# wo loaded in rows of 32 KB by two queues and turned on VectorE, with a reordered chain between the layers, in a cached decode of two attention and two FFN layers

## The chip, the cores and the metric

The kernel runs on one core of a Trainium2 chip (trn2). The metric is the device time of one launch in microseconds (us). Three runs of the kernel before took 293.29, 294.82 and 295.31 us, median 294.82.

## What is computed

One token of each of four sequences (B = 4, D = 512) goes through attention, FFN, the same attention again with the same caches and weights, and the same FFN again. K and V caches hold 8 heads of 4096 positions of 128 numbers for each sequence, in bf16; 32 query heads share them four by four.

```python
def _A_ref(x, k_cache, v_cache, wq, wo):
    q = (x @ wq).reshape(B, Sq, Hq, Dh).transpose(0, 2, 1, 3)
    k = jnp.repeat(k_cache, rep, axis=1)
    v = jnp.repeat(v_cache, rep, axis=1)
    scores = jnp.einsum("bhqd,bhkd->bhqk", q, k) * (Dh ** -0.5)
    p = _softmax(scores, axis=-1)
    o = jnp.einsum("bhqk,bhkd->bhqd", p, v)
    return o.transpose(0, 2, 1, 3).reshape(B, Sq, Hq * Dh) @ wo

def _B_ref(x, w_gate, w_up, w_down):
    return (_gelu(x @ w_gate) * (x @ w_up)) @ w_down

x = A_x
x = x + _A_ref(_layernorm(x), A_k_cache, A_v_cache, A_wq, A_wo)
x = x + _B_ref(_layernorm(x), B_w_gate, B_w_up, B_w_down)
x = x + _A_ref(_layernorm(x), A_k_cache, A_v_cache, A_wq, A_wo)
x = x + _B_ref(_layernorm(x), B_w_gate, B_w_up, B_w_down)
```

A K or V head of one sequence is 1 MiB. wq and wo are 4 MiB each, the three FFN weights 1.75 MiB each.

## The kernel before

The sequences (batches 0 to 3 in the code) are worked through one after the other, and each of them through layer 0 and layer 1 (the two passes; `L` in the names). For a batch the eight K heads are loaded once and stay in SBUF for both layers. V heads are loaded for layer 0 and again for layer 1, but for the heads in `HELD` (line 22), which stay. K and V heads share twelve slots of 1 MiB (`KV`); at the very end the four parts of wq, which is then no longer needed, serve as four more.

The order of the work is made by a planner in the kernel's own code (class `Plan`). Each step is a node with an engine, an assumed duration and the nodes it needs. `run` picks the order on each engine and the slot of each load; `LEAD`, `PATIENCE` and the `DMA_` numbers at the top steer it. The instructions are then emitted in this fixed order, and each engine works through its own in order. All loads but that of x are issued by SP in the order wq, K of batch 0, the first half of wo, V of batch 0, the second half of wo, w_gate, w_up, w_down in two halves, and then for each further batch its K, its V for layer 0, and the V of the batch before it for layer 1. A load into a slot waits on SP until the last reader of the slot's old content is done: for a slot of K these are the score products of layer 1 (`sc`, line 415), for a slot of V the values products (`val`, line 485).

The steps that the change and the prediction touch:

- K heads are turned in place before the scores, six of eight by VectorE (`turn`, line 366) and heads 5 and 7 by TensorE (line 373) with ScalarE's copies (`kcopy`, line 379).
- Scores of four heads at a time (z = 0 and 1) go to `S_ps` (line 415). Softmax: maximum (line 421) and bias (lines 429 to 432) on VectorE, exp on ScalarE (line 438), a turn of the result (line 447) on VectorE, a swap on TensorE (line 455), a copy on ScalarE (line 463).
- Values: head by head in two halves of 16 products of 128 weights each, into `O_ps` (line 485); `oscale` (line 493) divides by the softmax sum and writes `OT`.
- Output projection (`proj` line 613, `half_out` 632, `half_sum` 639, `proj_last` 623): heads grouped by `groups`, into `R_ps`; `addback` (lines 646 and 647) turns the result and adds it to XT, the residual, which is held with D on the partitions.
- Layer norm (`ln_sq` line 500, `ln_mm` 506, `ln_mid` 512 and 513, `ln_var` 521 and 522, `ln_root` 529 and 530): squares on VectorE, then one product with a matrix of 1/512 for the sums of x and of its squares together, then mean, difference and variance on VectorE, and the root on ScalarE.
- FFN: `up` (line 655) for gate and up, `ffturn` (line 662), GELU on VectorE and ScalarE (lines 678 to 707), `down` (line 715), `addback`.
- Query of layer 1: `qmm` (line 538) in two halves, `qevac` on ScalarE (line 551), `qturn` (line 556), `qsplit` (line 595), `qrep` (line 605), `expand` (line 392).
- `rows` (lines 727 and 728) turns the residual for the output, `leave` (line 732) adds the last FFN and writes out.

Line 1004 holds products that only keep TensorE busy; their results are not read.

Of the kernel before, what the change touches and what calls it, by code (L numbers as in the profile page):

```python
# [21 lines left out]
HELD = ((), (7,), (7,), (7,))  # L22
HALVES = {(b, 1, j) for b in range(3) for j in range(8)} | {(3, 1, 6)}
# [7 lines left out]
DMA_FETCH = 1.5  # L31
DMA_LEAD = 4.0

PATIENCE = (0.5, 1.5, 0.7)
LEAD = {"tn1": -3, "val0": 1, "sc10": -2, "chain": 2, "sc11": -6, "sm00": 1, "os0": -6, "op": -2, "sm01": 11, "sm10": 10, "qx1": 4, "other": 5, "sc00": 2, "sm11": 8, "os1": -4, "tn0": -2, "sc01": 1}
EARLY = {("pt", 1): 60.0, ("su", 1): 60.0}
WINDOW = 3.413
WARM = 0.45
FILL = 0.7
SPIN = 0.22  # L40
STREAM = {"sc": 0.85, "qm": 0.85, "up": 0.75, "up2": 0.75, "kt": 0.21, "pw": 0.16, "qp": 0.11, "qn": 0.05,
          "su": 0.02, "lnm": 0.03, "xt": 0.1, "ys": 0.2, "dn": 0.38, "dn2": 0.38}


def stage(n):
# [13 lines left out]
    if n[0] in ("lnq", "lnm", "lnc", "lnv", "lnr", "up", "ft", "ga", "gb", "gy", "gc", "zz", "dn", "da", "qm", "qe",  # L59
                "qt", "qn", "qc", "qk"):  # L60
        return "chain"
# [3 lines left out]
class Plan:  # L65
# [149 lines left out]
    def warm(self, places):  # L215
# [3 lines left out]
        for n, _ in self.order:  # L219
# [16 lines left out]
            past.append((z, last, 0.72 * d if kind == "val" else d - 0.15 if kind in ("op", "op2") else STREAM.get(kind, 0.0)))  # L236
# [4 lines left out]
def kernel(  # L241
# [22 lines left out]
    FT = F // 4  # L264
    scale = float(Dh) ** -0.5
# [237 lines left out]
    def ln_mm(bs, nb):  # L503
        def emit():
            st = R_ps[1][:, 0:2 * CD * nb].rearrange("p (s k b) -> p s k b", s=2, k=CD)
            nc.tensor.matmul(st, lhsT=ones_mean, rhs=XS[:, :, :, bs], start=True, stop=True)
        return emit

    def ln_mid(bs, nb):
        def emit():  # L510
            st = R_ps[1][:, 0:2 * CD * nb].rearrange("p (s k b) -> p s b k", s=2, k=CD)
            nc.vector.tensor_reduce(out=mu[:, :, 0:nb], in_=st, axis=AX.X, op=ALU.add)
            nc.vector.tensor_tensor(out=xn[:, :, bs], in0=XT[:, :, bs],
                                    in1=mu[:, 0, 0:nb].unsqueeze(1).broadcast_to([P, CD, nb]),
                                    op=ALU.subtract)
        return emit

    def ln_var(nb):
        def emit():
            t = lt[:, 0:nb]  # L520
# [12 lines left out]
    def qmm(z, bs, nb):  # L533
# [7 lines left out]
        return emit  # L541

# [46 lines left out]
    def qsplit(z, b):  # L589
        def emit():  # L590
            if b:
# [17 lines left out]
    def proj(src, nb, heads, first, last):  # L609
        def emit():  # L610
            for j in heads:
                for i in range(4):
                    nc.tensor.matmul(R_ps[0][32 * i:32 * i + nb, :], lhsT=src[:, 4 * j + i, 0:nb],  # L613
# [4 lines left out]
    def proj_last(src, nb, heads, last):  # L618
        def emit():
            todo = [4 * j + i for j in heads for i in range(4)]  # L620
            for h in todo:
                for t in range(4):
                    nc.tensor.matmul(R_ps[1][32 * t:32 * t + nb, 0:P], lhsT=src[:, h, 0:nb],  # L623
# [36 lines left out]
    def ffturn(z):  # L660
        def emit():
            nc.vector.transpose(out=PD[:, 0:FT].rearrange("p (c x) -> p c x", c=CF),  # L662
                                in_=R_ps[z][:, 0:FT].rearrange("p (r c) -> p c r", c=CF))
        return emit

    def ff(nb):
        n = CF * nb
        at, ah = (0, n) if nb > 1 else (992, 984)
        d = PD[:, 0:FT].rearrange("p (c x) -> p c x", c=CF)[:, :, 0:nb]
        u = PD[:, FT:FT + n].rearrange("p (c b) -> p c b", c=CF)  # L670
        g = PF[:, at:at + n].rearrange("p (c b) -> p c b", c=CF)
# [19 lines left out]
    def gelu_y(nb, y):  # L691
        def emit():
            d, g, u, h = ff(nb)
            if nb == 1:
                nc.vector.scalar_tensor_tensor(out=g, in0=g, scalar=y, in1=d, op0=ALU.mult, op1=ALU.mult)
            else:
                nc.vector.tensor_tensor(out=g, in0=g, in1=y.unsqueeze(1).broadcast_to([P, CF, nb]),
                                        op=ALU.mult)
                nc.vector.tensor_tensor(out=g, in0=g, in1=d, op=ALU.mult)
        return emit  # L700

    def gelu_c(nb):
        def emit():
# [3 lines left out]
            nc.vector.tensor_tensor(out=h, in0=g, in1=u, op=ALU.mult)  # L707
        return emit

    def down(nb, k):  # L710
        def emit():
            h = ff(nb)[3]
            for c in range(7 * k, 7 * k + 7):
# [12 lines left out]
    def rows():  # L726
        nc.vector.tensor_copy(out=xp[:, :, 0:B], in_=XT)
        nc.vector.transpose(out=xrow.rearrange("p (r c) -> p c r", c=CD), in_=xp)
# [14 lines left out]
    def groups(b, L):  # L743

        g = [[0, 1, 2, 3], [4, 5], [6], [7]]
        if L:
            g = [[7], [6, 5, 4], [3, 2, 1, 0]] if b < B - 1 else [[0], [1, 2, 3], [7], [4, 5], [6]]
        return g
# [14 lines left out]
    def loads_v(b, L):  # L763
        heads = [j for j in sum(groups(b, L), []) if not (L and j in HELD[b])]
        for i, j in enumerate(heads):
# [19 lines left out]
            if halves:  # L785
                for m in range(2):
                    pl.load(name + (m,), 4.1, ld_part(name, m, src), rd[m], soft=soft[m], half=True)
# [6 lines left out]
    def ld_wo(n):  # L794
        return lambda pick: nc.sync.dma_start(
            out=wo_sb[:, 16 * n:16 * n + 16],
            in_=A_wo[2048 * n:2048 * n + 2048].rearrange("(h p) n -> p h n", p=P))

    def ld_wd(k):
        return lambda pick: nc.sync.dma_start(  # L800
            out=wd_sb[:, 7 * k:7 * k + 7], in_=B_w_down.rearrange("(q c) n -> q c n", q=P)[:, 7 * k:7 * k + 7])

    pl.load("x", 0.5, ld_x, None)
    pl.load("wq", 32, plain(wq_sb[:], A_wq, "(q c) n -> q c n"), None)
# [4 lines left out]
    pl.load("wg", 14, plain(wg_sb[:], B_w_gate, "(q c) n -> q c n"), None)  # L809
# [242 lines left out]
```

## Time and profile before

| | us |
|---|---|
| median of three runs | 294.82 |
| profiled execution | 291.89 |
| its span (first to last instruction) | 290.1 |
| TensorE products busy, of which line 1004 | 236.3, 67.7 |
| VectorE busy | 133.5 |
| ScalarE busy | 74.5 |

The profile is of one execution. Engines are PE (TensorE products), PEld (its weight loads), DVE (VectorE), ACT (ScalarE) and SP, which issues the loads here; "SPq" or "ACTq" is the issuing instruction itself. Times are us from the span's start. A row of the chain of waits has start, duration and what it was; the chain is followed back from the last instruction. A row of a group has the line, engine and operation, the tiles and shapes, the count, then busy us and mean ns of one, and then the idle time before them with what ended it. A row of a stretch has from and to, its length, the busy time of the engines with the number of instructions, the granted TensorE clock, the share of time in which the DMA engines were busy, and what they moved in GB/s. The share can be a little over 1, since packets of one DMA engine overlap. The line of digits has forty slices of 7.25 us, in tenths.

### The profile page before, as it was taken

To read this page: it belongs to the slowest core of one execution; us is meant where nothing else is said; L and a number is where in the kernel's file an instruction comes from. 1 tells how busy PE (TensorE), PEld (TensorE's weight loads), DVE (VectorE), ACT (ScalarE), POOL (GpSimd) and SP (SyncE) were. 2 spreads that over 40 slices of the span, in tenths; PEclk is the share of its full clock that TensorE was granted. 3 is DMA by queue.
4 is the path that set the end of the run, shared out by engine and by line. 5 is a ranking of instruction groups with operands and counts; after the bars stand their busy time and mean duration, and the time that the engine had idled before them with its cause. 6 is when DMAs were issued, how large, how long until landed. Compare 5 with 4: busy or idle time off the path is not lost.

```text
span 290.1 us, 9733 instructions
## 1 busy us (share of the span) xinstructions
PE 236.3 (81%) x4419; PEld 138.3 (48%) x4419; DVE 133.5 (46%) x380; ACT 74.5 (26%) x167; POOL 0.7 (0%) x6
## 2 busy tenths in 40 slices
PE   4988887878687888798888698879977889897794
PEld 1433454443233565455434465554445655565552
DVE  4149911002289942052389721343998213444034
ACT  1020751001023852101224731000338321113010
POOL 0000000000000000000000000000000000000000
PEclk9999999999999999999999999999999999999999
DMA  7999999999999999999999999999999999999910
GB/s 312 412 421 419 376 405 416 414 371 426 415 407 395 419 421 417 402 407 406 393 417 416 425 416 411 405 407 390 413 422 416 408 387 403 396 382 420 411 47 1
DMA packets 21657, 112.04 MB, mean 386 GB/s; under 512 B 2032, under 2 KB 6128, under 8 KB 12272
## 3 DMA queue, kind: packets, MB, share of 16 engines
q1 hardware_dynamic: 21568, 111.42, 95.3%
q8 instruction: 34, 0.56, 0.8%
q14 instruction: 7, 0.06, 0.0%
q10 hardware_dynamic: 48, 0.01, 0.0%
HBM read 111.42 MB, written 0.00 MB: 384 GB/s over the span
## 4 chain that ended last, share of the span: by engine, by line
DMA 62%; PE 16%; SPq 11%; DVE 7%; issue 2%; ACT 1%; DVEq 0%
DMA KV<-in_A_v_cache_dram 43%; DMA KV<-in_A_k_cache_dram 8%; SPq L351 7%; PE O_ps L485 7%; DMA wd_sb<-in_B_w_down_dram 6%; DMA wq_sb<-in_A_v_cache_dram 5%; SPq L741 3%; PE S_ps L415 3%; DVE KV L366 2%; PE R_ps L715 1%; PE R_ps L538 1%; DVE PA L662 1%; PE S_ps L1004 1%; PE R_ps L655 1%; DVE sm L421 1%
## 5 line engine op out<-in xcount | busy, mean ns | idle before, releaser
L485 PE MATMUL O_ps<-PA,KV 128*128 128x56 bf16 x1920 | 66.3, 188 | 20.8 <-DMA KV<-in_A_v_cache_dram 17.3
L485 PEld LDWEIGHTS <-KV 128*128 128x128 bf16 x1920 | 57.6, 97 | 40.8 <-DMA KV<-in_A_v_cache_dram 32.4
L1004 PE MATMUL S_ps<-iden_b 128*128 128x512 bf16 x226 | 67.7, 401 | 3.6 <-DVE iden_b L321 3.6
L366 DVE STREAM_TRANSPOSE KV<-KV 128x1024 int32<-128x1024 int32 x48 | 56.5, 1214 | 0.6 <-DMA KV<-in_A_k_cache_dram 0.4
L379 ACT ACTIVATE KV<-R_ps 128x512 bf16<-128x512 f32 x64 | 34.9, 595 | 28.0 <-PE R_ps L373 27.9
L415 PE MATMUL S_ps<-KV,PA 128*32 128x512 bf16 x384 | 35.3, 394 | 2.1 <-DVE KV L366 1.3
L1004 PEld LDWEIGHTS <-iden_b 128*128 128x128 bf16 x227 | 21.9, 107 | 27.6 <-issue 11.7
L373 PE MATMUL R_ps<-iden_b,KV 128*128 128x128 bf16 x256 | 22.1, 219 | 6.3 <-ACT KV L379 3.1
L421 DVE TENSOR_REDUCE sm<-S_ps 128x1 f32<-128x512 f32 x16 | 10.8, 677 | 27.4 <-PE S_ps L415 27.4
L373 PEld LDWEIGHTS <-KV 128*128 128x128 bf16 x256 | 15.8, 97 | 14.8 <-issue 10.2
L415 PEld LDWEIGHTS <-PA 128*32 128x32 bf16 x384 | 11.4, 94 | 13.2 <-issue 4.4
L493 DVE TENSOR_TENSOR OT<-O_ps,XS 128x4 bf16<-128x4 f32 (+1 forms) x12 | 2.0, 164 | 32.9 <-PE O_ps L485 32.9
L415 PE MATMUL S_ps<-KV,QN 128*32 128x512 bf16 x128 | 16.8, 381 | 0.2 <-ACT KV L379 0.2
L438 ACT ACTIVATE PA<-S_ps,sm 128x512 bf16<-128x512 f32 x16 | 11.7, 732 | 20.4 <-DVE sm L432 17.6
L632 ACT ACTIVATE PA<-R_ps 128x256 f32<-128x256 f32 x10 | 3.8, 384 | 46.2 <-PE R_ps L613 41.1
L529 ACT ACTIVATE sm<-sm 128x1 f32<-128x1 f32 (+1 forms) x10 | 2.0, 203 | 52.6 <-DVE sm L522 52.6
L493 DVE TENSOR_TENSOR OT<-O_ps,rdk 128x16 bf16<-128x16 f32 (+3 forms) x18 | 3.1, 170 | 26.7 <-PE O_ps L485 26.7
L463 ACT ACTIVATE PA<-T_ps 128x512 bf16<-128x512 f32 x16 | 9.6, 597 | 13.0 <-PE T_ps L455 11.8
L556 DVE STREAM_TRANSPOSE PA<-PA 128x256 int32<-128x256 int32 x10 | 4.4, 437 | 14.9 <-ACT PA L551 14.2
L613 PE MATMUL R_ps<-wo_sb,OT 128*1 128x512 bf16 (+1 forms) x124 | 8.7, 378 | 2.6 <-DMA wo_sb<-in_A_wo_dram 1.4
L646 DVE STREAM_TRANSPOSE PA<-R_ps 128x128 f32<-128x128 f32 x9 | 2.9, 317 | 16.5 <-PE R_ps L623 10.2
L447 DVE STREAM_TRANSPOSE PA<-PA 128x256 int32<-128x256 int32 x16 | 7.0, 434 | 7.5 <-ACT PA L438 7.5
(92 smaller groups left out, 173.9 us busy)
## 6 DMA issues: line engine op xcount, KB each, us to landing
KV<-in_A_v_cache_dram SPq DMA_DIRECT2D x34, 1024.0 KB, 15.0
KV<-in_A_k_cache_dram SPq DMA_DIRECT2D x32, 1024.0 KB, 13.5
KV<-in_A_v_cache_dram SPq DMA_DIRECT2D x46, 512.0 KB, 7.0
wq_sb<-in_A_wq_dram SPq DMA_DIRECT2D x1, 4096.0 KB, 12.2
wo_sb<-in_A_wo_dram SPq DMA_DIRECT2D x2, 2048.0 KB, 19.5
wq_sb<-in_A_v_cache_dram SPq DMA_DIRECT2D x4, 1024.0 KB
wg_sb<-in_B_w_gate_dram SPq DMA_DIRECT2D x1, 1792.0 KB
wu_sb<-in_B_w_up_dram SPq DMA_DIRECT2D x1, 1792.0 KB
```

The source lines that it names most:

```text
L351: nc.sync.dma_start(out=where[name], in_=src.rearrange("(p c) d -> p (c d)", p=P))
L366: nc.vector.transpose(out=w, in_=w)
L373: nc.tensor.matmul(R_ps[k % 2][:, P * u:P * u + P], lhsT=where[name][:, at:at + P], rhs=iden_b[:], start=True, stop=True)
L379: nc.scalar.activation(out=where[name][:, 512 * k:512 * k + 512], in_=R_ps[k % 2][:], func=ACT.Copy)
L415: nc.tensor.matmul(S_ps[z][32 * t:32 * t + 32], lhsT=w, rhs=k, start=(m == 0 and x == 0), stop=(m == 1 and x == 3))
L421: nc.vector.tensor_reduce(out=cms[:, z:z + 1], in_=S_ps[z][:].rearrange("p c r -> p (c r)"), axis=AX.X, op=ALU.max)
L438: nc.scalar.activation(out=PW[L][z].rearrange("p (a r e) -> p a r e", a=8, e=2), in_=S_ps[z][:].rearrange("p (a e) r -> p a r e", e=2), fu ...
L463: nc.scalar.activation(out=PW[L][z], in_=T_ps[z][:].rearrange("p t x -> p (t x)"), func=ACT.Copy)
L485: nc.tensor.matmul(Ov[L][:, j], lhsT=vw[:, c, :], rhs=w[:, c // 2, :, c % 2].unsqueeze(1).broadcast_to([P, WIDE, 4]), start=(m == 0 and c ...
L613: nc.tensor.matmul(R_ps[0][32 * i:32 * i + nb, :], lhsT=src[:, 4 * j + i, 0:nb], rhs=wo_sb[:, 4 * j + i, :], start=(first and j == heads[0 ...
L741: return lambda pick: nc.sync.dma_start(out=dst, in_=src.rearrange(pat, q=P))
L1004: nc.tensor.matmul(sinks[place].rearrange("p (a n) -> p a n", a=4), lhsT=iden_b[:], rhs=every, start=True, stop=True)
```

## The change

- wo is laid out in SBUF in another way. Before, partition p held row p of each of the 32 query heads, so that a load took rows of 1 KB. Now partition 32q + h gets the 32 rows 32q to 32q + 31 of head h, 32 KB without a gap, and a quarter q is one load into 32 partitions. SP issues quarters 0 and 2 before V of batch 0; ScalarE issues quarters 1 and 3 behind a one-column activation that reads K head 6. Eight instructions on VectorE then turn blocks of 32 by 32 (heads against rows) in place, each 1024 words of 4 bytes with a step of 1 KB, which gives the old layout. The projections of batch 0 wait for all eight. In VectorE's fixed order the first of the eight stands ahead of the turn of the second softmax half of layer 0 (line 447), the others behind it and ahead of all `oscale` of layer 0.
- V head 7 of batch 0 stays for layer 1 too, as in the other batches. It is not loaded again. The loads for batch 1 get three slots (K heads 0 to 2) before those of K of batch 0 come free; before they got four.
- Layer norm takes two products: that of x needs only XT, that of the squares goes to the end of `O_ps[0]`.
- The first half of the query of layer 1 (batches 0 to 3) is left in PSUM and turned there by VectorE, and `qsplit` reads PSUM; the copy on ScalarE is gone for this half. In VectorE's order a K turn of the next batch stands between the variance and this turn.
- In the FFN the gate's GELU is finished first, and the up product is turned in two parts (8 and 6 of 14 chunks); each is multiplied and goes into its part of the down product. w_down is loaded in the same parts.
- The turn of the rows for the output stands behind the variance. Head groups of the last output projection are split further.
- Planner constants are changed, and with them the order of independent steps throughout.

```diff
-HELD = ((), (7,), (7,), (7,))
-HALVES = {(b, 1, j) for b in range(3) for j in range(8)} | {(3, 1, 6)}
+HELD = ((7,), (7,), (7,), (7,))
+HALVES = {(b, 1, j) for b in range(3) for j in range(7)} | {(3, 1, 6)}
...
-PATIENCE = (0.5, 1.5, 0.7)
+PATIENCE = (0.3, 1.5, 1.0)
...
+    CUT = (0, 8, CF)
...
+    def ln_place(s, nb):
+        return O_ps[0][:, 512 - CD * nb:] if s else R_ps[1][:, 0:CD * nb]
+
+    def ln_mm(s, bs, nb):
+        def emit():
+            st = ln_place(s, nb).rearrange("p (k b) -> p k b", k=CD)
+            nc.tensor.matmul(st, lhsT=ones_mean, rhs=XS[:, s, :, bs], start=True, stop=True)
+        return emit
+
+    def ln_sum(s, nb):
+        st = ln_place(s, nb).rearrange("p (k b) -> p b k", k=CD)
+        nc.vector.tensor_reduce(out=mu[:, s, 0:nb], in_=st, axis=AX.X, op=ALU.add)
...
+    def qturn_apart():
+        nc.vector.transpose(out=R_ps[0][:], in_=R_ps[0][:])
...
-    def ld_wo(n):
-        return lambda pick: nc.sync.dma_start(
-            out=wo_sb[:, 16 * n:16 * n + 16],
-            in_=A_wo[2048 * n:2048 * n + 2048].rearrange("(h p) n -> p h n", p=P))
+    wo_rows = A_wo.rearrange("(h q c) n -> q h (c n)", q=4, c=32)
+
+    def ld_wo(q, queue):
+        queue.dma_start(out=wo_sb[32 * q:32 * q + 32].rearrange("p c n -> p (c n)"), in_=wo_rows[q])
+
+    def wo_beside():
+
+        nc.scalar.activation(out=sm[:, 25:26], in_=where["k", 0, 6][:, 0:1], func=ACT.Copy)
+        for q in (1, 3):
+            ld_wo(q, nc.scalar)
+
+    def wo_turn(k):
+        def emit():
+            w = wo_sb[:].rearrange("p c n -> p (c n)").bitcast(I32).rearrange("p (c n) -> p n c", c=32)
+            w = w[:, 32 * k:32 * k + 32]
+            nc.vector.transpose(out=w, in_=w)
+        return emit
...
-    pl.load(("wo", 0), 20.5, ld_wo(0), None)
+    for q in (0, 2):
+        pl.load(("wo", q), 15.7, lambda pick, q=q: ld_wo(q, nc.sync), None)
+    add("wa", "ACT", 0.9, [("k", 0, 6)], wo_beside)
     loads_v(0, 0)
-    pl.load(("wo", 1), 20.5, ld_wo(1), None)
...
+    wo_ready = [add(("wt", k), "DVE", 2.16, [("wo", 0), ("wo", 2), "wa"], wo_turn(k)) for k in range(8)]
...
-            return [(h, [("os", b, 0, i), ("wo", h[0] // 4)]) for i, h in enumerate(g)]
+            return [(h, [("os", b, 0, i)] + wo_ready) for i, h in enumerate(g)]
...
+    def ffn(tag, a, bs, nb, y, clear=None):
+
+        one = nb == 1
+        g = [None, None]
+        for z, w in ((0, wg_sb), (1, wu_sb)):
+            g[z] = add(("up", tag, z), "PE", 0.93, [a, g[0], "wu" if z else "wg"], up(z, w, bs, nb), ins=32)
+        t0 = add(("ft", tag, 0), "DVE", 0.65, [g[0]], ffturn(0))
+        a = add(("ga", tag), "DVE", 0.59 if one else 0.72, [t0, ("lnr", ("f", tag))], gelu_a(nb, y))
+        e = add(("gb", tag), "ACT", 0.22 if one else 0.25, [a], gelu_b(nb))
+        if not one:
+            a = add(("gz", tag), "DVE", 0.28, [a], gelu_z(nb, y))
+        e = add(("gd", tag), "DVE", 0.72 if one else 0.95, [e, a], gelu_d(nb, y))
+        t1, h, n = a, None, None
+        for k in range(2):
+            t1 = add(("ft", tag, 1 + k), "DVE", (0.44, 0.36)[k], [g[1], t1], ffturn(1, k))
+            h = add(("gh", tag, k), "DVE", 0.18, [t1, e, h], gelu_h(nb, k))
+            if k and clear:
+                add(("zz", tag), "DVE", 0.07, [h], clear)
+            n = add(("dn", tag, k), "PE", (0.55, 0.42)[k], [h, n, ("wd", k)], down(nb, k), ins=8 * (CUT[k + 1] - CUT[k]))
+        return n
```

More of the change, by code (lines that the diff above doesn't have):

```diff
@@ L519, in emit @@
         def emit():
+            ln_sum(1, nb)
             t = lt[:, 0:nb]
@@ L607, in qrep, with proj @@
         return emit
-    def proj(src, nb, heads, first, last):
+    def proj(src, cols, nb, heads, first, last):
         def emit():
```

172 lines of the change are left out of this document (84 added, 88 removed).

## The prediction

> **What bounds the kernel now.** I read the page's second and third part first.
>
> ```profile
> DMA  7999999999999999999999999999999999999910
> GB/s 312 412 421 419 376 405 416 414 371 426 415 407 395 419 421 417 402 407 406 393 417 416 425 416 411 405 407 390 413 422 416 408 387 403 396 382 420 411 47 1
> ```
>
> The 16 DMA engines are busy in all slices but the first and the last two: the kernel is one stream, in the order in which SP issues it, and then a tail of some 12 us without DMA. Two slices dip without going idle (376, 371), so I looked at those stretches by themselves.
>
> ```profile
> core 0: us, PE busy (x) PEld busy (x) DVE busy (x) ACT busy (x) POOL busy (x), PEclk, DMA share, GB/s
> 5.00:10.00 5.00, 4.87 (x29) 1.81 (x27) 1.27 (x8) 0.41 (x2) 0.00 (x0) 1.00 1.04 446
> 33.00:37.00 4.00, 3.35 (x48) 2.18 (x46) 2.92 (x5) 4.00 (x9) 0.00 (x0) 1.00 1.10 352
> 42.00:57.00 15.00, 12.69 (x251) 7.59 (x246) 2.33 (x9) 1.38 (x3) 0.00 (x0) 1.00 1.01 418
> 59.00:63.00 4.00, 3.12 (x44) 1.84 (x43) 0.16 (x1) 0.00 (x0) 0.00 (x0) 1.00 1.09 348
> 86.00:89.00 3.00, 2.22 (x34) 1.00 (x26) 2.57 (x9) 1.05 (x3) 0.00 (x0) 1.00 0.86 339
> 36.00:64.00 28.00, 23.29 (x391) 13.58 (x390) 2.65 (x11) 5.86 (x12) 0.00 (x0) 1.00 1.04 400
> ```
>
> The last column is the rate. 5 to 10 us is wq (rows of 32 KB), 33 to 37 and 59 to 63 the halves of wo (rows of 1 KB), 42 to 57 V heads (rows of 8 KB). From 86 to 89 us the engines are really short of work (share 0.86). Why they are is in the chain of waits and in SP's own row.
>
> ```profile
> 61.10 17.76 DMA wd_sb<-in_B_w_down_dram
> 78.90 0.59 PE R_ps L715 x28
> ...
> 80.07 0.18 DVE XS L500
> 80.29 0.40 PE R_ps L506 x2
> ...
> 82.22 0.61 ACT PA L551
> 82.85 0.46 DVE PA L556
> ...
> 84.33 2.31 DVE KV L366 x2
> 86.64 0.59 DVE sm L421
> ```
>
> ```profile
> 86.42 3.08 SPq L351 DMA_DIRECT2D KV<-in_A_k_cache_dram  x4
> ```
>
> This is the point on which everything hangs. All 12 slots are full: K of batch 0 holds eight until both layers' scores are done, the first four K heads of batch 1 hold the rest. SP issues the fifth only at 86.42, when the second score product of layer 1 ends. That product comes 7.5 us after the second half of w_down landed (78.90), and w_down lands when 29.25 MiB (wq 4, K 8, wo 4, V 8, the three FFN weights 5.25) have passed. So: release = landing of w_down + 7.5 us. What is issued behind the release is a fixed amount, and the end follows the release.
>
> **The change, part by part.**
>
> *wo in rows of 32 KB.* The 4.19 MB lie ahead of w_down before and after. At 350 GB/s they take 12.0 us; at wq's 446 they would take 9.4, at the 418 of 8 KB rows 10.0. I take 9.7, so w_down lands 2.3 us earlier (2.0 to 2.6), at 76.6. This supposes that a transfer into 32 partitions runs like one into 128; no row shows such a transfer, and the first rival is about that.
>
> *Two quarters on ACT's queue.* The new node stands in ACT's order behind 14 of the 16 copies of turned K.
>
> ```profile
> 34.53 4.87 ACT L379 ACTIVATE KV<-R_ps 128x512 bf16<-128x512 f32 x9
> ```
>
> So it runs at 39.4. With one more us of issue and first bytes, quarters 1 and 3 start at about 41, beside the V heads that SP has queued. Alone they would take 4.7 us, at an equal share of the engines 9.4: they land between 46 and 51, I take 48.5. The last two copies wait behind this node for under 1 us; the scores that need them, and all that follows them on PE, come later by at most that, with V loads queued until 52: nothing.
>
> *Eight transpositions of wo on VectorE.* No row shows one that strides by 1 KB on both sides. The nearest:
>
> ```profile
> L366 DVE STREAM_TRANSPOSE KV<-KV 128x1024 int32<-128x1024 int32 x48 | 56.5, 1214 | 0.6 <-DMA KV<-in_A_k_cache_dram 0.4 <-issue 0.2
> ...
> L646 DVE STREAM_TRANSPOSE PA<-R_ps 128x128 f32<-128x128 f32 x9 | 2.9, 317 | 16.5 <-PE R_ps L623 10.2 <-PE R_ps L715 6.3
> ...
> L728 DVE STREAM_TRANSPOSE PA<-PA 128x128 f32<-128x128 f32 x1 | 0.4, 408 | 0.0
> ```
>
> Of the same size, unstrided: 1.21 us. L646 reads with a stride, L728 writes with one, and L728 takes 91 ns longer for 128 elements, which is 0.73 us for 1024. So 1.21 (stride free), 1.94 (write pays), 2.67 (both pay); I take 1.94, since L646 pays nothing visible for its stride. Eight are 15.5 us (9.7 to 21.4). VectorE is idle for it (2.65 us busy between 36 and 64), but in its order stand behind them the turn of the second softmax half (0.43, between the first and the second), and all scalings of the outputs of layer 0. They end at 48.5 + 0.4 + 15.5 = 64.4. From there the path to the second half of the down product has: scaling 0.2, values of head 6 (they wait for that scaling, both on O_ps) 1.1, the first two projections 1.7, then from head 7 on what batch 3 shows in the chain without a wait for weights:
>
> ```profile
> 241.54 1.04 PE O_ps L485 x32
> 242.58 0.68 PE R_ps L623 x32
> ...
> 250.03 0.57 PE R_ps L715 x26
> ```
>
> That is 9.1 us from 241.54 to 250.60, plus some 1.5 us because the two half sums and one more projection now stand behind head 7: 13.6 in all, so 78.0 against 76.6 + 0.5 = 77.1 if w_down sets it. In batch 3 PE took values of another head between these steps, some 0.4 us of it in the path, which I take off: I put 0.5 us on the path (0 with free strides, 5.7 with 2.67 us each). The break-even is 1.9 us a piece; every 0.1 us above costs 0.8. A second place: PE's swap of that softmax half waits behind the first transposition (about 51.3), and the slots of V heads 5 to 7 behind it; the stream has work until about 54.3 and gets V head 5 issued at about 53. That is just enough; if not, up to 1 us.
>
> *V head 7 of batch 0 kept.* One load (2.5 us at 418 GB/s) less. But the slot it keeps is the one that K head 3 of batch 1 had. Ahead of the release the stream now has one MiB less to move, and behind it the same 73 MiB as before. The stall at 86 to 89 grows by what the load saved: net 0. It pays only as far as the release itself comes earlier (bounds -2.5 and +0.5).
>
> *Layer norm in two products, query turned in PSUM, gate ahead.* The sum product starts with the row of XT instead of its square: 0.2 us (80.07 to 80.29) earlier, in every chain. The query's copy and turn (0.61 + 0.46) become one turn in PSUM of 512 elements, about 0.7 by
>
> ```profile
> L662 DVE STREAM_TRANSPOSE PA<-R_ps 128x448 f32<-128x448 f32 x10 | 6.5, 648 | 7.2 <-PE R_ps L655 7.1
> ```
>
> but a 1.2 us K turn stands ahead of it in VectorE's order, behind the later variance steps, and ends about 0.6 us after the query product; before, ACT's copy hid this. 0.3 saved, 0.6 waited: nothing, or -0.3. Gate ahead changes the order of the same steps; turning the up product in two parts adds about 0.1 us and lets the first 8 of 14 down chunks start earlier: even. Per chain -0.2, in the release too.
>
> *Later stalls.* Slices of 402, 390, 387, 396 and 382 GB/s fall where batches 2 and 3 wait for the same kind of release. V in halves explains about 407; what is below is worth some 2.6 us in all. Four chains that are 0.2 shorter and a new order give perhaps -0.5 (between -2.6 and +1: planner constants were changed, and any order can lose).
>
> *The tail.*
>
> ```profile
> 280.68 0.17 DVE XS L500
> 280.85 0.10 DVE PA L727
> 280.97 0.41 DVE PA L728
> 281.38 0.17 DVE sm L512
> ...
> 281.81 0.96 PE R_ps L655 x16
> ...
> 286.12 0.98 PE R_ps L715 x56
> ```
>
> L727 and L728 stand in the chain; now the copy falls into the product's time, and the turn behind the variance. The reduction starts 0.3 us earlier. From the gate product to the end of the down product it was 5.3 us; with the new order I count 5.4. Tail: -0.25.
>
> **Sum.** -2.3 (wo) + 0.5 (transpositions) + 0 (head 7) - 0.2 (chain ahead of the release) - 0.5 (later) - 0.25 (tail) = -2.75 us. The profiled execution took 291.89 us (span 290.1), so its like would take 289.1; it stood 2.9 below the median of the three runs, and on that median, 294.82, the sum gives 292.1.
>
> **The rivals.**
>
> *A quarter of the partitions takes half the rate.* Every large transfer in this trace fills 128 partitions. If a transfer into 32 reaches only half of the paths into SBUF, the rate is 223 instead of 446 and a quarter takes 4.7 us instead of 2.35. SP's quarters run alone between 32 and 41 us, ACT's start as they end, so "two at once" doesn't happen. SP's two then lose 4.7 us for sure, ACT's two lose between 0 and 4.7, as V rows fill in or not. w_down lands 2.4 to 7.1 later than now; the transpositions are hidden then. 294.82 + 4.7 - 0.95 = 298.6 (296.3 to 301). It decides from 290 GB/s over wo downward. Against it: nothing in the trace. The Trainium skill, page "SBUF — State Buffer", section "Door 1: The DMA port swizzle", gives 189 GB/s for 1 MiB into partitions 0 to 31 and 328 into 128, because 32 partitions reach 8 of 16 ports, and says under "Can I just issue two DMAs to hit both halves?" that a second transfer adds 6%; by that, this rival is the outcome. No run here shows it yet.
>
> *The transpositions come late.* With 2.4 us each the path gains 3.7 instead of 0.5: 295.3. Speaks for it: two strided sides. Against it: L646.
>
> *Head 7 pays.* If the release comes earlier than I have it (weights landing sooner, the path shorter), the stall doesn't grow and 2.5 us are kept: 289.6. For it: only 7.5 us lie between landing and release, of which 2.3 is K turns ahead of the scores.
>
> **How the numbers follow.** Forecast 0.45, half rate 0.26, head 7 pays 0.17, late transpositions 0.12. The time is the forecast's, 292.1, its own range 290.4 to 293.8. The range for 8 in 10 runs from 288.9 (head 7 pays, a little more) to 298.6 (the middle of the half rate). The runs before spread over 0.7%, so less than 1% can't be told from no change: faster means under 291.87, slower over 297.77. The forecast lies at that edge: 0.22 faster, 0.23 the same. With head 7 (0.17) faster is 0.39; with 0.08 of the late transpositions the same is 0.31; the half rate and the rest of the late ones are slower, 0.30.
>
> **What would show it.** wo: its stretch at 420 to 446 GB/s, w_down's products at about 77; half rate: a stretch near 220 from 32 us on, with DMA share at 1. Transpositions: a group of 8 near 1.94 us, ending near 64. Head 7: one load less, and the stretch behind K head 2 of batch 1 idle for about 3 us. Tail: the turn of the rows no longer ahead of the reduction. The forecast is wrong if the release is not 1.5 to 2.5 us earlier than 86.4, or if the stretch behind it is not the same length.

## The result, and the profile after

The changed kernel is slower. Its median is 306.58 us (305.41 to 307.13, four runs) against 294.06 us of the kernel before in the same comparison; the ratio is 1.0458, with a 95% interval of 1.0418 to 1.0497. The forecast was 292.1 us, its range ended at 298.6. The profiled execution took 307.13 us with a span of 305.2; before, the span was 290.1.

First the DMA rows and the clock row of the profile after, in 40 slices of 7.63 us.

```profile
PEclk9999988559999999999999799999997999999999
DMA  8999998999996899999999999999999999899920
GB/s 318 398 421 426 290 251 180 273 398 366 427 417 283 309 418 422 413 410 408 400 404 424 417 418 417 408 389 343 421 414 422 413 413 394 320 394 416 413 79 2
```

The DMA engines are as busy as before, but in slices 5 to 8 (30.5 to 61 us) they move 290, 251, 180 and 273 GB/s. A high share of busy time with 180 to 290 GB/s instead of some 420 is the first thing to see: the engines did not wait for work, their packets were slow. Slices 13 and 14 (283, 309) are another matter: there the share falls as well. The same places as stretches (from and to, length, busy times, clock, share, GB/s):

```profile
5.00:10.00 5.00, 4.79 (x35) 1.99 (x33) 1.33 (x9) 0.42 (x2) 0.00 (x0) 1.00 1.01 433
...
50.00:58.00 8.00, 0.00 (x0) 0.00 (x0) 0.00 (x0) 0.00 (x0) 0.00 (x0) 0.57 0.95 196
60.00:65.00 5.00, 4.31 (x73) 3.24 (x71) 5.00 (x4) 0.60 (x1) 0.00 (x0) 0.50 1.01 419
97.00:100.00 3.00, 2.82 (x58) 1.47 (x55) 2.66 (x5) 0.18 (x1) 0.00 (x0) 1.00 0.10 38
```

wq, 32 KB rows into 128 partitions, runs at 433 GB/s. From 50 to 58 us ScalarE's quarters of wo and some V rows run at 196 with a share of 0.95, and TensorE does nothing. At 60 the stream is back at 419; at 97 to 100 it is dry. Now the chain of waits of the same stretch, and the group and SP rows that belong to it.

```profile
40.35 19.13 DMA wo_sb<-in_A_wo_dram
...
61.82 0.30 DVE PA L448
62.13 14.63 DVE wo_sb L842 x7
...
78.31 21.29 DMA KV<-in_A_k_cache_dram
```

```profile
L842 DVE STREAM_TRANSPOSE wo_sb<-wo_sb 128x1024 int32<-128x1024 int32 x8 | 16.9, 2192 | 14.3 <-DMA wo_sb<-in_A_wo_dram 14.3
```

```profile
L846 SPq DMA_DIRECT2D wd_sb<-in_B_w_down_dram x2: 432/454/475, 71.7 to 72.2; - x2
...
DMA to landing us min/median/max: 18.6/19.3/20.0
```

```profile
99.73 5.70 SPq L352 DMA_DIRECT2D KV<-in_A_k_cache_dram  x5
```

ScalarE's quarters, issued at 40.0, land at 59.5. The transpositions take 2.19 us each and end at 76.8. SP issues the second half of w_down at 72.2, and it lands 20.0 later, at 92.2 instead of 78.9. The release (the load that waits for the last score product of layer 1) comes at 99.73 instead of 86.42: 13.3 us later, of the 15.1 by which the span grew. The chain as printed runs from wo through the transpositions to a K head whose slot comes free behind them, and so seems to blame the transpositions; the run without them, below, says how much of the time they make.

### The profile page after: what moved, and what is told of

It reads as the page before. It is cut to its first block, busy times and chain, and to the rows that moved or that the text cites. A ratio compares the mean times of both kernels' runs of the same rounds, so it can differ in the third digit from the quotient of the medians.

```text
span 305.2 us, 9824 instructions
## 1 busy us (share of the span) xinstructions
PE 239.0 (78%) x4451; PEld 147.3 (48%) x4451; DVE 152.0 (50%) x409; ACT 71.7 (23%) x164; POOL 0.7 (0%) x6
## 4 chain that ended last, share of the span: by engine, by line
DMA 65%; PE 17%; DVE 11%; issue 3%; ACT 2%; SPq 0%; ACTq 0%; DVEq 0%
DMA KV<-in_A_v_cache_dram 36%; DMA KV<-in_A_k_cache_dram 19%; PE O_ps L486 7%; DMA wo_sb<-in_A_wo_dram 6%; DVE wo_sb L842 6%; DMA wq_sb<-in_A_wq_dram 4%; PE S_ps L416 4%; PE R_ps L374 2%; DVE KV L367 1%; ACT KV L380 1%; PE R_ps L746 1%; PE R_ps L637 1%; PE R_ps L557 1%; DVE sm L422 1%; PE R_ps L647 1%
## 5 line engine op out<-in xcount | busy, mean ns | idle before, releaser
L486 PE MATMUL O_ps<-PA,KV 128*128 128x56 bf16 x1920 | 68.1, 190 | 33.2 <-DMA KV<-in_A_v_cache_dram 26.1
L486 PEld LDWEIGHTS <-KV 128*128 128x128 bf16 x1920 | 60.7, 98 | 51.1 <-DMA KV<-in_A_v_cache_dram 34.4
L1059 PE MATMUL S_ps<-iden_b 128*128 128x512 bf16 x227 | 63.4, 396 | 3.6 <-DVE iden_b L322 3.6
L416 PE MATMUL S_ps<-KV,PA 128*32 128x512 bf16 x384 | 36.8, 416 | 2.3 <-DVE PA L393 1.8
L374 PE MATMUL R_ps<-iden_b,KV 128*128 128x128 bf16 x256 | 23.9, 231 | 6.5 <-DMA KV<-in_A_k_cache_dram 4.3
L842 DVE STREAM_TRANSPOSE wo_sb<-wo_sb 128x1024 int32<-128x1024 int32 x8 | 16.9, 2192 | 14.3 <-DMA wo_sb<-in_A_wo_dram 14.3
L374 PEld LDWEIGHTS <-KV 128*128 128x128 bf16 x256 | 17.3, 103 | 13.7 <-issue 6.7
L494 DVE TENSOR_TENSOR OT<-O_ps,rdk 128x4 bf16<-128x4 f32 (+2 forms) x19 | 3.2, 166 | 17.2 <-PE O_ps L486 17.2
L688 DVE STREAM_TRANSPOSE PA<-R_ps 128x448 f32<-128x448 f32 (+2 forms) x15 | 7.3, 490 | 6.0 <-PE R_ps L679 6.0
L469 PEld LDWEIGHTS S_ps<-mask_th,sm 128*128 128x128 f32 x32 | 4.8, 187 | 10.6 <-ACT PA L439 10.6
L469 PE MATMUL S_ps<-mask_th,sm 128*128 128x16 f32 x32 | 6.2, 269 | 4.8 <-ACT PA L439 4.6
```

The lines of the kernel that those rows point to most:

```text
L374: nc.tensor.matmul(R_ps[k % 2][:, P * u:P * u + P], lhsT=where[name][:, at:at + P], rhs=iden_b[:], start=True, stop=True)
L416: nc.tensor.matmul(S_ps[z][32 * t:32 * t + 32], lhsT=w, rhs=k, start=(m == 0 and x == 0), stop=(m == 1 and x == 3))
L469: nc.tensor.matmul(S_ps[z][:, 0, 0:16], lhsT=sms[:, z:z + 1].broadcast_to([P, P]), rhs=mask_th[:].rearrange("p t h -> p (t h)"), start=Tru ...
L486: nc.tensor.matmul(Ov[L][:, j], lhsT=vw[:, c, :], rhs=w[:, c // 2, :, c % 2].unsqueeze(1).broadcast_to([P, WIDE, 4]), start=(m == 0 and c ...
L688: nc.vector.transpose(out=PD[:, 32 * c0:32 * c1].rearrange("p (c x) -> p c x", x=32), in_=R_ps[z][:, 0:FT].rearrange("p (r c) -> p c r", c ...
L842: nc.vector.transpose(out=w, in_=w)
```

## The experiments

Theory A: a transfer into 32 neighbouring partitions runs at half rate. Theory B: the wait for wo and its transpositions costs the time. Ratios are against the kernel before, run beside each kernel. "Release" is SP's issue as above. Each kernel is the changed one in its own order with only what is named altered, but for four: two hold transfers alone, one is the kernel before with the wo part, and one has another plan for V head 7.

**wo as one transfer.**

```diff
-        queue.dma_start(out=wo_sb[32 * q:32 * q + 32].rearrange("p c n -> p (c n)"), in_=wo_rows[q])
+        if q == 0:
+            queue.dma_start(out=wo_sb[:].rearrange("p c n -> p (c n)"), in_=wo_rows)
```

ScalarE's two loads are deleted.

> As the changed kernel, in the same order of instructions, but wo comes as one transfer of 4 MiB from SP's queue into all 128 partitions, in the same rows of 32 KB, ahead of V of batch 0; ScalarE issues nothing of it. Theory A (a transfer into 32 partitions runs at half rate, and V rows beside it too; in the changed kernel's trace the stream moves 200 to 230 GB/s from 32 to 58 us): wo moves at 440 GB/s from 32 to 42 us, w_down has landed at 75.3 us (77.6 before, 89.4 in the changed kernel) and the release, the issue of K head 3 of batch 1 (99.7 in the changed kernel), comes at 84.2 to 85.5; with the 205.5 us behind it that gives 291 to 293 us. Theory B (the eight transpositions, now 2.19 us each, and what waits for them set the release; there are 40.2 us from the landing of wo to the release): the transpositions end at 59 to 60 us, but the release stays behind the weights, later than 90 us, and the time is over 297.

Measured: 357.41 us, ratio 1.2176 (1.2117 to 1.2236). Neither theory had the reason ("over 297" of theory B covers the number alone). The DMA row and a stretch of this kernel's trace:

```profile
DMA  8999992222223999799999999999999999999940
```

```profile
60.00:100.00 40.00, 0.00 (x0) 0.00 (x0) 0.00 (x0) 0.00 (x0) 0.00 (x0) 0.50 0.25 61
```

wo alone ran for 40 us with a share of 0.25, that of four engines out of sixteen, and 61 GB/s, 15 for each of the four. The source pattern has the four quarters as its outermost step. The Trainium skill, page "DMA: Bandwidth & Descriptors", section "Why a DMA increments its semaphore by 16 and not by 1", says that the number of engines is the largest up to 16 that divides the slowest dimension of both patterns: four here, and the share agrees. So this run is no test of either theory, but it holds a hint: each of the four engines moved little more than half of what each of sixteen moves in wq (433 / 16 = 27 GB/s).

**All four quarters on SP.**

```diff
-        pl.load(("wo", q), 15.7, lambda pick, q=q: ld_wo(q, nc.sync), None)
+        pl.load(("wo", q), 15.7, lambda pick, q=q: [ld_wo(q + i, nc.sync) for i in range(2)], None)
```

ScalarE's two loads are deleted.

> As the changed kernel, but all four quarters of wo are issued by SP, one after the other ahead of V of batch 0; ScalarE issues none. Theory A in its narrow form (only the quarters themselves run at half rate): wo takes 18.8 us instead of 9.4, nothing runs beside it, V of batch 0 then moves at 418 GB/s, w_down lands at about 84.5 us, 5 us earlier than in the changed kernel, where the V rows of ScalarE's two quarters were slowed as well: about 301.5 us. Theory B: wo has landed at 51.5 us instead of 59.5, the release comes 8 us earlier: 298.5. If two queues at once had been a help, this kernel would be slower than the changed one: over 307.

Measured: 304.26 us, ratio 1.0356 (1.0300 to 1.0412), release at 96.66.

```profile
34.00:52.00 18.00, 10.72 (x83) 5.15 (x81) 2.27 (x6) 6.48 (x14) 0.00 (x0) 0.77 0.99 206
55.00:65.00 10.00, 6.26 (x94) 4.47 (x95) 8.41 (x5) 0.60 (x1) 0.00 (x0) 0.54 1.01 412
```

With nothing beside them the quarters run at 206, and V comes at 412 as soon as they are through. Theory A in its narrow form had the mechanism, but 2.8 us too little: w_down landed 3.1 us earlier than in the changed kernel, not 5. This run alone does not part the theories, since wo landed at 56.5 us (not 51.5), 3.0 earlier than in the changed kernel, and a release that follows wo would have come 3 us earlier too. The next run parts them. "Two queues at once" was no help: its release comes 3.1 us later than this one.

**Without the transpositions.**

```diff
-            nc.vector.transpose(out=w, in_=w)
```

> As the changed kernel with its four quarters on two queues, but the eight transpositions of wo on VectorE are left out, so wo stays in the layout in which it was loaded and the output is not the reference's. Theory A: w_down lands no more than 0.5 us earlier than at 89.4 and the time is that of the changed kernel, 306.6, or up to 1 us less. Theory B: what waits behind the last quarter's landing is 17 us shorter, V heads 5 to 7 and the FFN weights are issued up to 6 us earlier, and the release comes 6 us earlier or more: 300 or less.

Measured: 305.54 us, ratio 1.0434 (1.0358 to 1.0511), release at 98.14, 1.6 us earlier than with them. Theory B asked for 6 or more; it falls as the main cause. Theory A missed too, by less: it allowed 0.5 us. In time the two kernels can't be told apart (1.0434 with 1.0358 to 1.0511, against 1.0458), so the 1.6 us are those of two traces. They begin with the wait behind the first transposition: PE's swap comes 0.55 us later with it (62.18 against 61.63 us), and the values of the third head 1.7 later (67.19 against 65.46); TensorE's granted clock is 0.50 until 68 us with the transpositions and until 64 without. SP waits for the values before it can issue V heads 5 to 7.

**wo in rows of 1 KB again**, both halves ahead of V, no transpositions.

```diff
-        queue.dma_start(out=wo_sb[32 * q:32 * q + 32].rearrange("p c n -> p (c n)"), in_=wo_rows[q])
+        n = q // 2
+        queue.dma_start(out=wo_sb[:, 16 * n:16 * n + 16],
+                        in_=A_wo[2048 * n:2048 * n + 2048].rearrange("(h p) n -> p h n", p=P))
...
-            nc.vector.transpose(out=w, in_=w)
```

ScalarE's two loads are deleted.

> As the changed kernel in the same order of instructions, but wo comes in the old layout: two halves in rows of 1 KB from SP's queue, now both ahead of V of batch 0, without transpositions. It tells what all the rest of the change (V head 7 kept, layer norm in two products, query turned in PSUM, gate ahead, new order) is worth. By the sum of the prediction the rest gives -0.45 to -0.95 us: 293.1 to 293.6. By the changed kernel's own trace, where 205.5 us lie behind the release instead of 203.7, and 10.2 instead of 8.9 us between the landing of w_down and the release, the rest costs up to 3 us: 295 to 297.

Measured: 294.27 us, ratio 1.0045 (1.0014 to 1.0076), release at 86.91. The rest of the change costs 1.3 us (0.4 to 2.2) instead of bringing 0.5 to 1.

**The rates alone.** The quarters of (1) and those of (7) differ in this alone:

```diff
-        queue.dma_start(out=flat[32 * q:32 * q + 32], in_=rows[q])
+        nc.sync.dma_start(out=flat[q:P:4], in_=rows[q])
```

> Only transfers, none of the computation: twelve loads of 4 MiB or 2 MiB in turn, each behind the landing of the one before, and an output of zeros, so its time is no time of the kernel's; the rates in its trace are what is read. The order is: (0) 128 partitions from one contiguous stretch, rows of 32 KB; (1) the changed kernel's four quarters on one queue; (2) four quarters of 32 partitions, each from a contiguous MiB; (3) quarters 0, 2 on SP's queue beside 1, 3 on ScalarE's; (4) 0, 1 beside 3, 2; (5) two V heads; (6) quarters 1, 3 on ScalarE's queue beside two V heads on SP's; (7) as (1), but into every fourth of the 128 partitions; (8) 128 partitions, rows 128 KB apart in a K cache; (9) two transfers into 64 partitions, contiguous; (10) halves of wo in rows of 1 KB. Why a packet of 32 KB takes 2.4 to 2.5 us in the quarters and 1.21 in wq is open; the run of wo as one transfer showed 2.4 us too, with only some four engines at work. Theory A1 (a block of 32 neighbouring partitions is what limits): 200 to 225 GB/s for (1) and (2), 420 to 446 for (0), (7), (8) and (9) (at least 300). Theory A2 (rows 128 KB apart in HBM are what limits): 200 to 225 for (1), (7) and (8), 420 to 446 for (0), (2) and (9). If two queues at once help, (3) or (4) is over 300; if not, 200 to 230. For (6) a shared limit gives 200 to 230 while quarters are under way, separate ones over 300.

The stretches of its trace lie inside (0), (1), (2), (3), (4), (6), (7), (8), (9) and (10), in this order; VectorE and GpSimd are the busy columns, then clock, share and GB/s.

```profile
3.00:12.00 9.00, 0.00 (x0) 0.00 (x0) 1.00 0.94 408
16.00:34.00 18.00, 0.00 (x0) 0.00 (x0) 1.00 0.99 204
39.00:57.00 18.00, 0.00 (x0) 0.00 (x0) 1.00 0.96 198
62.00:80.00 18.00, 0.00 (x0) 0.00 (x0) 1.00 0.97 200
85.00:99.00 14.00, 0.00 (x0) 0.00 (x0) 1.00 0.97 213
110.00:123.00 13.00, 0.00 (x0) 0.00 (x0) 1.00 1.01 232
128.00:136.00 8.00, 0.00 (x0) 0.00 (x0) 1.00 0.99 426
141.00:149.00 8.00, 0.00 (x0) 0.00 (x0) 1.00 0.93 401
154.00:172.00 18.00, 0.00 (x0) 0.00 (x0) 1.00 0.94 195
176.00:186.00 10.00, 0.16 (x1) 0.00 (x0) 1.00 1.08 353
```

What decides is where the rows go, not where they come from: contiguous rows into 32 neighbours run at 198, the quarters' own rows into every fourth partition at 426, rows 128 KB apart into 128 partitions at 401. Two queues at once, in either pairing, give 200 and 213; V heads beside two quarters share the low rate (232 in all). Theory A1 held but for (9), where it asked for at least 300 and 64 neighbours are no better than 32 (195); (0) and (8), at 408 and 401, are also a little under the 420 that it asked for. The Trainium skill, page "SBUF — State Buffer", section "Door 1: The DMA port swizzle", has a rule for it: partitions 32 apart use the same port and partitions 64 apart do not, so 0 to 63 reach the same 8 of 16 ports as 0 to 31, while by its table every fourth partition reaches all 16; the rates agree. By that rule the rows h, 32 + h, 64 + h and 96 + h share two ports, which at the page's 27.2 GB/s a port would be 54 GB/s, an estimate; the one transfer, if it wrote these four side by side (no row shows its order), ran at 61, somewhat above. The same page's "Can I just issue two DMAs to hit both halves?" gives 6% for two transfers, one at partition 0 and one at 64; here the pairing across the halves (0 with 3, 1 with 2) gave 4% over one queue (213 against 204), the other one -2% (200).

**Only the wo part, on the kernel before.** The edit is the wo part of the diff above: the loads, the column on ScalarE, the transpositions, and the projections that wait for them.

> The kernel before with nothing but the wo part of the change: quarters of 32 KB rows, two on each queue, and eight transpositions on VectorE. If the loss is the wo part alone, it is 11 to 14 us slower than before: 304 to 307. If it needs the rest of the change as well (three K heads instead of four ahead of the release), it is 2.5 us or more under the changed kernel's 306.6, or it is within 6 us of before.

Measured: 305.65 us, ratio 1.0448 (1.0402 to 1.0494). The wo part alone carries the loss.

**V head 7 loaded a second time**, on the kernel with rows of 1 KB.

```diff
-HELD = ((7,), (7,), (7,), (7,))
-HALVES = {(b, 1, j) for b in range(3) for j in range(7)} | {(3, 1, 6)}
+HELD = ((), (7,), (7,), (7,))
+HALVES = {(b, 1, j) for b in range(3) for j in range(8)} | {(3, 1, 6)}
```

> As the run with wo in the old rows (294.27, ratio 1.0045), but V head 7 of batch 0 is loaded a second time, as before the change, so that four K heads of batch 1 come ahead of the release; the order is planned anew. If keeping the head is worth nothing, as the prediction had it: 294 to 294.6. If keeping it pays 2.5 us: 296 to 297. If it costs, because the stall ahead of the release grows by more than the load: 292 to 293.5, no slower than before.

Measured: 294.28 us, ratio 1.0042 (1.0014 to 1.0071), release at 86.70: keeping the head is worth nothing. The stretch around the release shows why, first with the head kept (the kernel with rows of 1 KB), then with it loaded:

```profile
84.00:91.00 7.00, 5.65 (x81) 2.56 (x81) 5.77 (x15) 1.05 (x3) 0.00 (x0) 1.00 0.56 212
```

```profile
84.00:91.00 7.00, 5.53 (x82) 2.42 (x78) 5.80 (x14) 1.05 (x3) 0.00 (x0) 1.00 0.95 369
```

212 instead of 369 GB/s over 7 us are 1.1 MB, just the one head that was not loaded.

**wo at full rate: three kernels.** The first takes the rows of wo as those of wq; the second deletes the transpositions as well; the third has the same load behind that of V head 3. In all three ScalarE's two loads are deleted.

```diff
+        if q == 0:
+            queue.dma_start(out=wo_sb[:].rearrange("p c n -> p (c n)"),
+                            in_=A_wo.rearrange("(p c) n -> p (c n)", p=P))
```

> As the changed kernel in the same order of instructions, but wo comes as one contiguous transfer of 4 MiB into 128 partitions (rows of 32 KB, as wq), from SP's queue ahead of V of batch 0, and the eight transpositions are kept. Partition p then holds rows 32p to 32p + 31, which is not the layout that the projections want, so the output is not the reference's; the time is that of a kernel whose wo comes at the rate that the prediction supposed. By the prediction's first three steps, on the 294.27 us of the run with rows of 1 KB: wo lands at 42, w_down 2.3 us earlier than there (77.7), at 75.4; the transpositions end at 60 and are hidden: 292.0 to 292.5, 0.5 to 1 us under before. If the stream's gain is lost again (a longer stall ahead of the release, or a path from the transpositions that sets it): 294 to 295.

> As the run before it, one contiguous transfer of wo, but without the eight transpositions; the output is not the reference's. If they are hidden when wo lands at 42 us, as the prediction's arithmetic gives (their end at 60, needed at about 64): the same within 0.4 us. If VectorE's order makes something wait behind them (the turn of the second softmax half, and with it V heads 5 to 7 in SP's queue): 1 to 3 us faster.

> As the first of these three, with the transpositions, but SP issues the one transfer of wo behind the first four V heads of batch 0, so that it lands at about 51.6 us; the output is not the reference's. By the prediction's path (13.6 us from the end of the transpositions to that of the down product, which starts behind w_down otherwise): transpositions from 52 to 69.5, down product at 83 instead of 77, so 5 to 7 us slower than the first of the three. If the chain behind the transpositions is shorter or other work fills it: under 3 us slower.

Measured: 292.93 us with the transpositions and 292.51 without, both at a ratio of 0.9985 (0.9954 to 1.0016); 301.69, ratio 1.0276 (1.0222 to 1.0330), with wo behind four V heads. The first one's w_down and release:

```profile
L846 SPq DMA_DIRECT2D wd_sb<-in_B_w_down_dram x2: 431/432/432, 56.4 to 56.8; - x2
...
DMA to landing us min/median/max: 18.7/19.4/20.1
```

```profile
84.39 5.86 SPq L352 DMA_DIRECT2D KV<-in_A_k_cache_dram  x5
```

Its second half of w_down lands 20.1 us after 56.8, at 76.9. Early transpositions are hidden. In the third kernel the release comes at 92.92, 8.5 us later than in the first, and this is where the time goes:

```profile
42.00:51.00 9.00, 2.76 (x41) 1.73 (x40) 0.58 (x4) 0.78 (x2) 0.00 (x0) 0.99 1.05 451
53.00:61.00 8.00, 4.51 (x54) 2.73 (x54) 7.04 (x5) 0.60 (x1) 0.00 (x0) 0.50 0.21 79
```

wo comes at 451 and then the stream is nearly dry for 8 us (79 GB/s instead of some 420 loses 6.5 of them): the turn of the second softmax half stands behind the first transposition on VectorE, PE's swap and the values behind that turn, the slots behind the values, and SP behind the slots. The expectation had the loss in another place, the path from the transpositions to the down product, and that path is at work too. The chain of waits of this trace runs along it:

```profile
56.44 14.63 DVE wo_sb L844 x7
...
85.83 0.47 PE R_ps L748 x24
```

The second half of the down product starts 14.8 us after the end of the transpositions (71.07) and 1.1 after w_down has landed (84.7). So the dry stream accounts for most of the 7.8 us by which w_down lands later, the path for 0.7 more, and which of the two would have held the release back alone this run does not tell.

**More filling products**, on the kernel with rows of 1 KB, which has TensorE's clock at half speed in three short stretches that the kernel before does not have.

```diff
-WARM = 0.55
+WARM = 0.95
```

> As the run with wo in rows of 1 KB (ratio 1.0045; its trace has the clock at 0.5 for 3.4 us from 49.3, 165.4 and 264.3 us, where the kernel before has it at full speed throughout), in the same order of instructions but for more of the products that only keep TensorE busy (the threshold that asks for them is 0.95 instead of 0.55, 64 products more). If the rest of the change loses its 1.2 us because TensorE is idle too long and its clock is halved behind that: the stretches at 0.5 go and the time falls to before's, 293.3, or under. If the loss lies in the new order itself: 294 or more, whether the stretches at 0.5 go or not.

Measured: 294.32 us, ratio 1.0039 (1.0006 to 1.0071). The clock rows of the kernel with rows of 1 KB and of this one:

```profile
PEclk9999998899999999999999899999999999997999
```

```profile
PEclk9999997799999999999999999977999999999999
```

The stretches moved and did not go, and the time stayed. Whether the clock is the cause is not settled by this.

**Pieces.** Can the quarters be kept and still get the rate?

> Only transfers of wo again, 4 MiB each in turn, and an output of zeros; the rates in the trace are what is read: (0) pieces of 32 partitions by 8 KB on one queue, blocks 0, 2, 1, 3 in turn; (1) the same pieces with blocks 0 and 1 on SP's queue beside 2 and 3 on ScalarE's; (2) two contiguous transfers into every second partition; (3) pieces of 2 KB a row, blocks in turn, on one queue. If what is limited is a single transfer's reach, and transfers close behind one another can use both halves of the paths: (0), (1) or (3) over 300 GB/s, and a version of the changed kernel with full rate would be possible. If neighbouring transfers don't overlap so: 200 to 230 in (0) and (1), no more in (3). (2) should be at 380 like every fourth partition (381 measured), against 203 for 64 neighbours.

```profile
4.00:8.00 4.00, 0.16 (x1) 0.00 (x0) 1.00 1.02 238
4.00:24.00 20.00, 0.16 (x1) 0.00 (x0) 1.00 1.02 228
30.00:38.00 8.00, 0.16 (x1) 0.00 (x0) 1.00 0.97 214
43.00:52.00 9.00, 0.00 (x0) 0.00 (x0) 1.00 0.94 408
56.00:83.00 27.00, 0.16 (x1) 0.00 (x0) 1.00 0.47 140
```

The first row lies in (0); ScalarE begins to issue its pieces of (1) at 7.66 us, so the second row holds both kinds. The third lies in (1), the last two in (2) and (3). Pieces of 8 KB give 238 in turn on one queue, and 228 and 214 with two queues at work; pieces of 2 KB give 140 with a share of 0.47, and SP's 64 issues last from 53.66 to 83.5 us, so the engines waited there for the issues. Every second partition runs at 408. No version of this layout came near the full rate, and no kernel of these beats the one before by more than a measurement can tell.

## Why the prediction was wrong

**Step 1, wo in 32 KB rows: wrong, and it decides.** The sentence that failed is "this supposes that a transfer into 32 partitions runs like one into 128". The 9.7 us taken for the 4.19 MB mean 432 GB/s; the quarters ran at 206, and w_down, which was to land 2.3 us earlier, landed 10.2 later with all of them on SP (89.1 instead of 78.9) and 13.3 later in the changed kernel. Where the rate was what the step supposed (429 GB/s from 34 to 41 us in the kernel at full rate), the step was right to 0.3 us: w_down landed at 76.9 (76.6 forecast), and the release came at 84.39, 2.0 before 86.42 (1.5 to 2.5 forecast).

The other half of that step, release = landing of w_down + 7.5, held but in the last row, where the path from the transpositions comes 0.7 us behind. The landing is the later issue of w_down plus the longer time to landing.

| kernel | w_down landed | release | between |
|---|---|---|---|
| before | 78.9 | 86.42 | 7.5 |
| after | 92.2 | 99.73 | 7.5 |
| quarters on SP | 89.1 | 96.66 | 7.6 |
| no transpositions | 90.6 | 98.14 | 7.5 |
| rows of 1 KB | 79.4 | 86.91 | 7.5 |
| full rate | 76.9 | 84.39 | 7.5 |
| full rate, late | 84.7 | 92.92 | 8.2 |

So the loss is in the stream ahead of w_down. Of the 15.3 us between the releases at full rate (84.39) and after (99.73), 12.3 are there with the quarters on SP alone, and 3.1 come from ScalarE's queue beside V. Of the 12.3 the rate itself makes 10.3: 4.19 MB take 20.6 us at the 204 GB/s of the rates' run and 10.3 at its 408. The transpositions behind a late wo made 1.6 in the changed kernel; the last 0.4 I can't assign.

**Step 2, ScalarE's quarters: wrong.** They started when forecast (40.3 against 41), but landed at 59.5, not 48.5. V rows beside them did not fill the gap: they took on the low rate.

**Step 3, transpositions: price within its bounds, wrong in one cover.** They took 2.19 us (1.94 taken, 1.21 to 2.67 allowed). By the step's own rule of 0.8 us for every 0.1 above 1.9 that is some 2.3 us on the path, not 0.5 (and 2.67 would be 6.2, not the 5.7 given). No run had wo landed at 48.5 us, as the step supposed: with wo at 42 they cost nothing, and with wo at 53.9 the path from their end to the end of the down product took 15.2 us (71.07 to 86.30) where the step counts 13.6. The second place was mis-sized: "up to 1 us" for V heads 5 to 7 behind PE's swap was far too little once wo is late, with 6.5 us of dry stream in the kernel with wo behind four V heads. The prediction's own margin there, about 1 us of queued loads, was too thin for a term of 1 us.

**Step 4, V head 7: right, and by its mechanism.** 294.27 with it kept, 294.28 with it loaded; the stall at the release grows by the one load saved.

**Step 5, layer norm and query: -0.2 forecast, not seen.** With rows of 1 KB and head 7 reloaded, the release comes at 86.70, 0.3 later than before.

**Step 6, later stalls: wrong sign, and so was the supposition that what lies behind the release has a fixed length.** At full rate the release is 2.0 us earlier, the time only 0.4 less by the ratio (1.4 less to 0.5 more). Stretches of that kernel and, 2 us later, of the kernel before:

```profile
180.00:207.00 27.00, 22.94 (x526) 14.56 (x530) 13.56 (x49) 3.15 (x10) 0.00 (x0) 1.00 1.01 388
...
232.00:260.00 28.00, 21.02 (x499) 13.54 (x495) 7.61 (x37) 2.99 (x9) 0.00 (x0) 0.94 0.98 379
```

```profile
182.00:209.00 27.00, 23.72 (x538) 14.65 (x539) 13.13 (x45) 3.96 (x12) 0.00 (x0) 1.00 1.02 403
...
234.00:262.00 28.00, 23.31 (x583) 15.45 (x584) 8.89 (x37) 3.76 (x11) 0.00 (x0) 1.00 1.02 394
```

388 instead of 403 over 27 us, and 379 instead of 394 over 28 us, are some 1.0 us each: the two stretches in which batches 2 and 3 wait for their releases give the gain back. They are not all of it. In these two executions 207.2 us lie behind the release instead of 203.7 (spans of 291.6 and 290.1), so 1.5 of the 3.5 us are not in the two stretches. Why the new order is worse stays open; clock and order were not told apart.

**Step 7, tail: right for the part that it names.** From the start of the last addback to the end of the last down product it was 280.12 to 287.10 before and is 295.17 to 301.87 now, 0.28 less; 0.25 was forecast. To the end of the span nothing is left of it in these two traces (10.0 us in both), since what follows the down product, the writing of the output, took 0.3 us longer.

```profile
280.12 0.33 DVE PA L646
```

```profile
295.17 0.33 DVE PA L670
...
300.82 1.05 PE R_ps L746 x56
```

**The rivals.** The half rate was the first rival, with its mechanism; its chance of 0.26 was too small, since a rule spoke for it and only the absence of a row against it. Its time was too small as well (298.6, at most 301, against 306.6): it let V rows fill in beside ScalarE's quarters, counted the transpositions as hidden, and carried the 0.95 us of steps 5 to 7 as a gain where the rest cost 1.3.

## What to carry to other kernels

A transfer's rate depends on which partitions it writes: 32 or 64 neighbours got half of what 128, every second or every fourth got, and neither a second queue nor smaller pieces made up for it, so a load that is to run at full rate should spread over the whole range of 128 partitions, all of them or every second or fourth, with an outermost dimension that all engines can share. Where a forecast rests on a shape that no row of the trace shows, that shape deserves the larger part of the chance. A load that stands ahead of others in one issue order should be tried for what its consumers hold up: a transposition that waits for its load, ahead of a small turn, left the stream nearly dry for 8 us.

## What was not expected of the hardware

A narrow transfer slows wide ones beside it: V heads and quarters together ran at 232 GB/s, in the kernel at 196, and at 419 once the quarters were through. One transfer into all 128 partitions whose outermost step was four used four engines and ran at 61 GB/s. And TensorE's granted clock fell to half while it had nothing to do and stayed there over the work behind that (0.57 from 50 to 58 us, 0.50 from 60 to 65), where the kernel before never fell under full speed ahead of its last microseconds.
